# First group's weight preparation reordered: ACT's raising and beginning of a weight put behind the step's activations, DVE's lower part put ahead of the join

## Chip, cores and metric

The kernel runs on one core of one Trainium2 chip. The metric is the time of one execution on the device, in microseconds (us). A program has one instruction queue for each engine: PE (matmuls), ACT, DVE, POOL, and SP, which here issues every DMA. An engine works its queue strictly in order, so an instruction that waits holds up all that stand behind it.

## What is computed

Attention with a window and block summaries, then a feed-forward layer on its result. Cut to what matters:

```python
# q, k, v: (4, 8, 768, 64); w_in: (512, 2048); w_out: (2048, 512); all float32
k_sum = k.reshape(B, H, 24, 32, D).max(axis=3)
v_sum = v.reshape(B, H, 24, 32, D).mean(axis=3)
scores = concat([where(|i - j| < 16, scale * q @ k.T, -1e9),
                 scale * q @ k_sum.T + log(32)], axis=-1)
x = (softmax(scores) @ concat([v, v_sum])).reshape(3072, 512)   # heads side by side
h = x @ w_in
out = (h * tanh(softplus(h))) @ w_out                            # (3072, 512)
```

Each float32 matmul is made of three faster ones, on operands that are split into a rounded high part and a low remainder: high by high, low by high, high by low.

## The kernel before

**Groups and steps.** The 3072 tokens are worked in six groups of 512. A group takes 16 steps, one for each slice of 128 of the 2048 inner columns. Step i, counted over all groups, runs `ff_in` for slice i (12 matmuls into one PSUM tile `ph`, L406), its activation `a` on ACT (`ff_act`, L413), the split of `a` into `ah` (by ACT in the first group, L422) and `al` (by DVE, L424), and `ff_out` for slice i-2 (12 matmuls `po`, L434), which reads `ah` and `al` of two steps before. PE also does the attention of the next group in between: in steps 0, 4, 8 and 12 of the first group the scores (`sc`, L311), in steps 3, 7, 11 and 14 the transposes `pt_ps` (L359), which ACT copies to `pt` (L361), and in steps 4, 8, 12 and 15 the products with the values, `x_ps` (L391), which read `pt`. Of the scores DVE makes `pr` and `nm` (eight instructions, L333), ACT the exponentials (eight, L337); one step later DVE takes the reciprocals `rs` (L347, L348) and POOL multiplies `pr` by them (L351). The exponentials and `a` use different ACT tables, so ACT loads a table on each change.

**Weights.** The weights come from memory as 64-bit floats, in 16 pieces of two slices; their order is w_in 0, 2, w_out 0, w_in 4, w_out 2, w_in 6, w_out 4, and so on, up to w_out 14. Here they are called pieces 0 to 15 (13 is w_in 14, 14 is w_out 12, 15 is w_out 14). Each goes through five small functions, one call of each in a step of the first group:

- `load_weight`: two DMAs of 512 KB into one of two staging tiles `w`; it waits until the piece two before has left that tile.
- `begin_weight`: ACT makes `f` (L136), DVE makes `x` (L138, L140), both from the staging tile.
- `join_weight`: DVE joins `f` and `x` in place (L148, L150).
- `upper_weight`: ACT rounds `f` to `w_hi` (L158).
- `lower_weight`: DVE makes `w_lo` = `f` - `w_hi` (L165).

The order is written by hand: the scheduler keeps the order in which the loop at L514 calls them, on each engine. Step i begins piece i+4, loads piece i+6 and joins piece i+3. Before the change it raises and lowers piece i+2, so that the raise at the head of step i waits for the join of step i-1. The last begin is in step 11, the last join in step 12. What SP issues in a step besides the weight are loads for the attention of later steps: `qk`, `vw` and `vm` in steps 4, 8, 12, and the sources `vsum` and `ks` of the summaries, one after the other through a single buffer (`ks` is read by DVE's `km`, L244, in steps 4, 6, 8, 10; `vsum` by `vq`, L264, in steps 5, 7, 9, 11).

Of the kernel before, what the change touches and what calls it, by code (L numbers as in the profile page):

```python
# [58 lines left out]
def fused_kernel(ctx: ExitStack, tc: tile.TileContext, q0, qk, kt, v0, vw, vs, w_in, w_out, out):  # L59
# [46 lines left out]
    def home(j, part, dtype, name):  # L106

        if j == NW:
            t = stage.tile([P, WB, WP], I64, tag="stage", name=name).bitcast(dtype)
            return t.rearrange("p k f -> p (k f)")[:, :WB * WP]  # L110
        pool = const if j < EARLY else late[0]
        return pool.tile([P, WB * WP], dtype, tag=f"w{part}_{j}", name=name, bufs=1)
# [6 lines left out]
    def load_weight():  # L119
        if weights:  # L120
            w, fc = weights.pop(0)
            t = stage.tile([P, WB, WP], I64, tag="stage", name=f"w{w}_{fc}")
            for k in range(WB):
                nc.sync.dma_start(t[:, k, :], (w_in, w_out)[w][fc + k])
            loaded.append((w, fc, t))

    def begin_weight():
        if loaded:
            w, fc, t = loaded.pop(0)
            j = order[w, fc]  # L130
            flat = t.rearrange("p k f -> p (k f)")
            high = flat.bitcast(U32).rearrange("p (f two) -> p f two", two=2)[:, :, 1]
            quarter = flat.bitcast(U16).rearrange("p (f four) -> p f four", four=4)
            x = home(j, 0, U32, f"x{w}_{fc}")
            f = home(j + 1, 1, F32, f"f{w}_{fc}")
            nc.scalar.activation(f, high.bitcast(F32), AF.Copy, scale=2.0 ** -OFFSET)  # L136
            half = x.bitcast(U16).rearrange("p (f two) -> p f two", two=2)
            nc.vector.tensor_scalar(out=half[:, :, 0], in0=quarter[:, :, 1], scalar1=13, scalar2=None,  # L138
                                    op0=ALU.logical_shift_right)
            nc.vector.tensor_scalar(out=half[:, :, 1], in0=quarter[:, :, 3], scalar1=SIGN, scalar2=None,  # L140
                                    op0=ALU.bitwise_and)
            begun.append((w, fc, f, x))

    def join_weight():
        if begun:
            w, fc, f, x = begun.pop(0)
            u = f.bitcast(U32)
            nc.vector.tensor_scalar(out=f, in0=f, scalar1=-_as_f32(F32_MAX), scalar2=_as_f32(F32_MAX),  # L148
                                    op0=ALU.max, op1=ALU.min)
            nc.vector.scalar_tensor_tensor(out=u, in0=u, scalar=3, in1=x,  # L150
                                           op0=ALU.logical_shift_left, op1=ALU.bitwise_or)
            joined.append((w, fc, f))

    def upper_weight():
        if joined:
            w, fc, f = joined.pop(0)
            split[w, fc, 0] = home(order[w, fc], 0, F32R, f"w{w}_{fc}_hi")
            nc.scalar.copy(split[w, fc, 0], f)  # L158
            raised.append((w, fc, f))

    def lower_weight():
        if raised:
            w, fc, f = raised.pop(0)
            split[w, fc, 1] = home(order[w, fc], 1, F32R, f"w{w}_{fc}_lo")
            nc.vector.tensor_sub(split[w, fc, 1], f, split[w, fc, 0].bitcast(F32))  # L165
# [177 lines left out]
    def att_normalize(group):  # L343
        n = len(group) * NQ
        u = units[group[0]]
        rs = small.tile([P, 2 * NQ], F32, tag="rs", name=f"rs{group[0][0]}_{group[0][1]}")[:, :n]
        nc.vector.tensor_scalar_add(rs, u["sm"][:, :n], 1e-9)  # L347
        nc.vector.reciprocal(rs, rs)  # L348
        if u.get("squares"):
            nc.gpsimd.memset(u["wide"][:, :, KA:], 0.0)  # L350
        nc.gpsimd.tensor_mul(u["pr"], u["pr"], rs.unsqueeze(2).broadcast_to([P, n, KA]))  # L351
# [23 lines left out]
    def att_values(group):  # L375
        c, hp0 = group[0]
        n = len(group)
        g, half = divmod(c, CG)
        if g not in xs:
            xs[g] = (xp.tile([P, HP, TG], F32R, tag="xh", name=f"xh{g}"),  # L380
                     xp.tile([P, HP, TG], F32R, tag="xl", name=f"xl{g}"))
        xh, xl = (x[:, hp0:hp0 + n, half * CH:(half + 1) * CH] for x in xs[g])
        ps = att_psum(c, f"x_ps{c}_{hp0}")
        for k, unit in enumerate(group):
            u = units.pop(unit)
            for s in range(NQ):
                for h in range(2):
                    d = slice(h * D, (h + 1) * D)
                    x = ps[d, k * CH + s * QT:k * CH + (s + 1) * QT]
                    pt = u["pt"][:, h * NQ // 2 + s // 2, s % 2 * QT:(s % 2 + 1) * QT]  # L390
                    nc.tensor.matmul(x, u["v"][:, s, d], pt, start=True, stop=True)  # L391
        x = ps[:, :n * CH].rearrange("p (k t) -> p k t", k=n)
        nc.scalar.copy(xh, x)  # L393
        return lambda: nc.vector.tensor_sub(xl, x, xh.bitcast(F32))  # L394
# [5 lines left out]
    def ff_in(g, fc):  # L400
        xh, xl = xs[g]
        ph = ps_w.tile([P, TG], F32, tag="w", name=f"ph{g}_{fc}")
        wh, wl = (weight(0, part, fc) for part in range(2))
        for cc in range(NCC):
            for n, (w, x) in enumerate(((wh, xh), (wh, xl), (wl, xh))):
                nc.tensor.matmul(ph, w[:, cc * P:(cc + 1) * P], x[:, cc, :],  # L406
                                 start=(cc == 0 and n == 0), stop=(cc == NCC - 1 and n == 2))
        st[g, fc] = ph

    def ff_act(g, fc):  # L410

        a = ff.tile([P, TG], F32, tag="t", name=f"a{g}_{fc}", bufs=2)
        nc.scalar.activation(a, st[g, fc], AF.Mish)  # L413
        st[g, fc] = a

    def ff_split(g, fc):

        a = st[g, fc]
        ah = ff.tile([P, TG], F32R, tag="ah", name=f"ah{g}_{fc}")
        al = ff.tile([P, TG], F32R, tag="al", name=f"al{g}_{fc}")  # L420

        (nc.scalar.copy if g == 0 else nc.vector.tensor_copy)(ah, a)  # L422
        st[g, fc] = ah, al
        return lambda: nc.vector.tensor_sub(al, a, ah.bitcast(F32))  # L424
# [87 lines left out]
    turned = {i + (3 if i < NFC - 4 else 2): group for i, group in at.items() if i < NFC - 1}  # L512
    following = dict(zip(turns, (at[i] for i in turns[1:])))
    for i in range(len(steps) + 2):  # L514
        upper_weight()
        join_weight()
        begin_weight()
        load_weight()
        if i - 1 in at and i < NFC:
            att_normalize(at[i - 1])  # L520
        if i < len(steps):
            ff_in(*steps[i])
            ff_act(*steps[i])
            if i < NFC:
                split_rest = ff_split(*steps[i])
        group = values.get(i)
        lower = att_values(group) if group else None
        if lower and i >= NFC:
            lower()
        if i in at:  # L530
            att_scores(at[i], i >= NFC - 1)
        lower_weight()
        if i < NFC:
            if lower:
                lower()
            split_rest()
        if i - 1 in at and i >= NFC:
            att_normalize(at[i - 1])
        if i - 3 in at and i - 3 >= NFC - 1:
            att_transpose_blocks(at[i - 3], 1)  # L540
        if NFC <= i < len(steps):
            ff_split(*steps[i])()
        if i - 2 in at and i - 2 >= NFC - 1:
            att_transpose_blocks(at[i - 2], 0)
        if i - 3 in following:
            n, m = following[i - 3]
            att_summarize_values(*m)
            after = todo.index(m) + 1
            if after < len(todo) and todo[after][0] % CPB == 0:
                load_key_source(todo[after][0] // CPB, todo[after][1])  # L550
        if i in following:
            n, m = following[i]
            att_summarize_keys(*n)
            for unit in (n, m):
                att_load_keys(*unit)
        if i - 1 in following:
            n, m = following[i - 1]
            att_summarize_values(*n)
            if m[0] % CPB == 0:
                load_key_source(m[0] // CPB, m[1])  # L560
        if i - 2 in following:
            n, m = following[i - 2]
            att_summarize_keys(*m)
            for unit in (n, m):
                att_block_keys(*unit)
        if group:
            for unit in at.get(i, ()):
                att_load_values(*unit)
        if i >= 2:
            ff_out(*steps[i - 2])  # L570
        if i in turned:
            att_transpose(turned[i])
# [44 lines left out]
```

## Time and profile before

| what | before |
|---|---|
| median of 3 runs | 634.47 us (633.5 to 635.5) |
| profiled execution, its own time | 633.05 us |
| its span, first to last instruction | 630.9 us |
| mean granted TensorE clock | 0.99 |
| PE matmul busy | 604.1 us, 96% of the span |
| DVE busy | 385.8 us, 61% |
| ACT busy | 258.8 us, 41% |
| POOL busy | 78.7 us, 12% |
| DMA | 69.26 MB, 110 GB/s over the span |

How to read it: busy shares are means over stages that differ. The span has a lead-in of some 45 us, the first group, which prepares the weights beside its own work, and five more groups in which the weights lie ready. Only the first group's steps are changed.

### The profile page before, as it was taken

To read this page: it belongs to the slowest core of one execution; us is meant where nothing else is said; L and a number is where in the kernel's file an instruction comes from. 1 tells how busy PE (TensorE), PEld (TensorE's weight loads), DVE (VectorE), ACT (ScalarE), POOL (GpSimd) and SP (SyncE) were. 2 spreads that over 40 slices of the span, in tenths; PEclk is the share of its full clock that TensorE was granted. 3 is DMA by queue.
4 is the path that set the end of the run, shared out by engine and by line. 5 is a ranking of instruction groups with operands and counts; after the bars stand their busy time and mean duration, and the time that the engine had idled before them with its cause. 6 is when DMAs were issued, how large, how long until landed. Compare 5 with 4: busy or idle time off the path is not lost.

```text
span 630.9 us, 10795 instructions
## 1 busy us (share of the span) xinstructions
PE 604.1 (96%) x4096; PEld 495.1 (78%) x4096; DVE 385.8 (61%) x1032; ACT 258.8 (41%) x630; POOL 78.7 (12%) x119
## 2 busy tenths in 40 slices
PE   5859999799999999999999999999999999999997
PEld 4747887588888888788888888888888888888886
DVE  4678999982855667855656758756647636222221
ACT  3759867675334244245144244153253251111111
POOL 4441020221011011011011010110110110000000
PEclk9979999999999999999999999999999999999999
DMA  8957587733223043533033241532232010100001
GB/s 273 319 191 249 215 271 238 220 115 97 92 72 122 2 146 122 169 98 97 0 98 96 92 147 55 169 99 88 75 97 82 16 33 0 68 0 1 0 1 66
DMA packets 31779, 69.26 MB, mean 110 GB/s; under 512 B 4720, under 2 KB 11120, under 8 KB 31728
## 3 DMA queue, kind: packets, MB, share of 16 engines
q1 hardware_dynamic: 31728, 68.58, 34.2%
q8 instruction: 32, 0.52, 0.4%
q14 instruction: 19, 0.16, 0.1%
HBM read 60.16 MB, written 6.29 MB: 105 GB/s over the span
## 4 chain that ended last, share of the span: by engine, by line
PE 78%; DMA 7%; DVE 7%; ACT 3%; issue 2%; SPq 1%; POOL 0%; DVEq 0%; ACTq 0%; POOLq 0%
PE po L434 37%; PE ph L406 35%; DMA vw<-vw 3%; PE x_ps L391 3%; PE sc L311 3%; DMA w<-w_out 2%; DMA w<-w_in 1%; DVE w_lo L165 1%; DVE al L424 1%; DVE x L138 1%; ACT f L136 1%; ACT pr L337 1%; DVE x L140 1%; DVE f L148 1%; DMA ks<-kt 1%
## 5 line engine op out<-in xcount | busy, mean ns | idle before, releaser
L413 ACT ACTIVATE a<-ph 128x512 f32<-128x512 f32 x96 | 57.2, 596 | 284.1 <-PE ph L406 230.6
L434 PE MATMUL po<-w_hi,ah 128*128 128x512 f32 x384 | 152.0, 396 | 0.7 <-ACT ah L422 0.5
L434 PE MATMUL po<-w_hi,al 128*128 128x512 f32 x384 | 149.9, 390 | 1.4 <-DVE al L424 1.4
L406 PE MATMUL ph<-xh,w_hi 128*128 128x512 f32 x384 | 150.7, 393 | 0.0
L406 PE MATMUL ph<-xl,w_hi 128*128 128x512 f32 x384 | 150.2, 391 | 0.0
L406 PE MATMUL ph<-xh,w_lo 128*128 128x512 f32 x384 | 150.0, 391 | 0.0
L434 PE MATMUL po<-w_lo,ah 128*128 128x512 f32 x384 | 149.6, 390 | 0.0
L422 DVE CAST ah<-a 128x512 fp32r<-128x512 f32 x80 | 34.6, 433 | 144.1 <-ACT a L413 143.6
L372 DVE STREAM_TRANSPOSE pt<-pr 32x256 f32<-32x256 f32 x256 | 111.5, 436 | 3.6
L434 PEld LDWEIGHTS po<-w_hi,ah 128*128 128x128 f32 x384 | 72.1, 188 | 19.0 <-issue 3.0
L434 PEld LDWEIGHTS po<-w_hi,al 128*128 128x128 f32 x384 | 72.1, 188 | 16.7 <-DVE al L424 2.5
L406 PEld LDWEIGHTS ph<-xh,w_hi 128*128 128x128 f32 x384 | 72.6, 189 | 15.2 <-issue 0.2
L406 PEld LDWEIGHTS ph<-xh,w_lo 128*128 128x128 f32 x384 | 72.5, 189 | 15.2
L406 PEld LDWEIGHTS ph<-xl,w_hi 128*128 128x128 f32 x384 | 72.5, 189 | 14.9
L434 PEld LDWEIGHTS po<-w_lo,ah 128*128 128x128 f32 x384 | 72.1, 188 | 15.2
L337 ACT ACTIVATE pr<-pr,nm 128x120 f32<-128x120 f32 x192 | 73.2, 383 | 14.8 <-DVE nm L333 14.6
L351 POOL TENSOR_TENSOR pr<-pr,rs 128x960 f32<-128x960 f32 (+1 forms) x28 | 47.4, 1692 | 221.8 <-DVE rs L348 131.8
L424 DVE TENSOR_TENSOR al<-a,ah 128x512 fp32r<-128x512 f32 x96 | 69.7, 726 | 5.9 <-ACT ah L422 3.1
L391 PEld LDWEIGHTS x_ps<-pt,vw 120*64 120x64 f32 x768 | 25.7, 141 | 21.3 <-issue 8.6
L391 PE MATMUL x_ps<-pt,vw 120*64 120x64 f32 x768 | 29.4, 229 | 12.7 <-ACT pt L361 5.4
L394 DVE TENSOR_TENSOR xl<-x_ps,xh 128x512 fp32r<-128x512 f32 (+1 forms) x28 | 17.2, 614 | 34.9 <-ACT xh L393 34.5
L337 ACT ACTIVATION_READ_ACCUMULATOR pr<-pr,nm 128x1 f32 x192 | 35.9, 187 | 0.0
(59 smaller groups left out, 451.4 us busy)
## 6 DMA issues: line engine op xcount, KB each, us to landing
qk<-qk SPq DMA_DIRECT2D x40, 496.0 KB, 4.1
vw<-vw SPq DMA_DIRECT2D x48, 192.0 KB, 5.1
w<-w_in SPq DMA_DIRECT2D x16, 512.0 KB, 5.2
w<-w_out SPq DMA_DIRECT2D x16, 512.0 KB, 5.2
ks<-kt SPq DMA_DIRECT2D x16, 384.0 KB, 4.4
out<-o SPq DMA_DIRECT2D x24, 256.0 KB, 2.3
vsum<-vs SPq DMA_DIRECT2D x12, 384.0 KB, 3.4
vw<-vm SPq DMA_DIRECT2D x40, 48.0 KB
```

Of the source, the lines that this page charges most:

```text
L136: nc.scalar.activation(f, high.bitcast(F32), AF.Copy, scale=2.0 ** -OFFSET)
L311: nc.tensor.matmul(ps[h][row, at0:at0 + KA], u["qk"][r, s, h * QT:(h + 1) * QT], u["qk"][r, s, P:], start=True, stop=True)
L337: nc.scalar.activation(pr[:, j, :], pr[:, j, :], AF.Exp, scale=-1.0, bias=nm[:, j:j + 1], accum_out=sm[:, j:j + 1])
L351: nc.gpsimd.tensor_mul(u["pr"], u["pr"], rs.unsqueeze(2).broadcast_to([P, n, KA]))
L372: nc.vector.transpose(u["tr"][b * SQ:(b + 1) * SQ, :, a * SQ:(a + 1) * SQ], u["wide"][a * SQ:(a + 1) * SQ, :, b * SQ:(b + 1) * SQ])
L391: nc.tensor.matmul(x, u["v"][:, s, d], pt, start=True, stop=True)
L394: return lambda: nc.vector.tensor_sub(xl, x, xh.bitcast(F32))
L406: nc.tensor.matmul(ph, w[:, cc * P:(cc + 1) * P], x[:, cc, :], start=(cc == 0 and n == 0), stop=(cc == NCC - 1 and n == 2))
L413: nc.scalar.activation(a, st[g, fc], AF.Mish)
L422: (nc.scalar.copy if g == 0 else nc.vector.tensor_copy)(ah, a)
L424: return lambda: nc.vector.tensor_sub(al, a, ah.bitcast(F32))
L434: nc.tensor.matmul(po[g][t], a[:, tok], w, start=(fc == 0 and n == 0), stop=(fc == NFC - 1 and n == 2))
```

## The change

Three calls move within the body of the step loop; the functions themselves stay as they are.

```diff
     for i in range(len(steps) + 2):
-        upper_weight()
+        lower_weight()
         join_weight()
-        begin_weight()
-        load_weight()
         if i - 1 in at and i < NFC:
             att_normalize(at[i - 1])
         if i < len(steps):
...
         if i in at:
             att_scores(at[i], i >= NFC - 1)
-        lower_weight()
+        begin_weight()
+        load_weight()
+        upper_weight()
         if i < NFC:
             if lower:
                 lower()
```

After it, a step's ACT work is: activation, `ah`, the copy of `x_ps`, the exponentials, then `f` of piece i+4 and the raise of piece i+3, which waits for the join of the same step. DVE starts a step with the lower part of piece i+2, then joins piece i+3, takes the reciprocals and the scores, and only then makes `x` of piece i+4. The load of piece i+6 stands at the same place in SP's queue as before.

The first place is on ACT, around the end of step 11 (`a_11`; numbers of heads and of w_in or w_out are left out of the names: the first `w_14_hi` is piece 13, `w_12_hi` piece 14, `f_14_1443` piece 15). Before:

```order
L158 CAST w_14_hi<-f_14_1339 128x1024
L136 ACTIVATE f_14_1443<-w_14_1343 128x1024
L413 ACTIVATE a_11_1460<-ph_11_1447 128x512
L422 CAST ah_11_1462<-a_11_1460 128x512
L361 COPY pt_0_1485<-pt_ps_0_1486 120x512
L361 COPY pt_0_1485<-pt_ps_1_1492 120x512
L158 CAST w_12_hi<-f_12_1395 128x1024
L413 ACTIVATE a_12_1515<-ph_12_1502 128x512
L422 CAST ah_12_1517<-a_12_1515 128x512
```

And the same stretch of ACT's queue with the change:

```order
L158 CAST w_14_hi<-f_14_1363 128x1024
L413 ACTIVATE a_11_1457<-ph_11_1444 128x512
L422 CAST ah_11_1459<-a_11_1457 128x512
L136 ACTIVATE f_14_1463<-w_14_1367 128x1024
L158 CAST w_12_hi<-f_12_1415 128x1024
L361 COPY pt_0_1487<-pt_ps_0_1488 120x512
L361 COPY pt_0_1487<-pt_ps_1_1494 120x512
L413 ACTIVATE a_12_1517<-ph_12_1504 128x512
L422 CAST ah_12_1519<-a_12_1517 128x512
```

The activation of step 11 has moved ahead of one `f`; the two copies of the transposes have moved behind that `f` and behind the raise of piece 14. Steps 3 and 7 read the same.

The second place is on DVE, from the end of step 0's scores into step 1 (`w_0_lo` is piece 2, `w_4_lo` piece 3, `f_2` and `x_2` piece 4, `x_6` piece 5). Before:

```order
L165 TENSOR_TENSOR w_0_lo<-f_0_651,w_0_hi 128x1024
L424 TENSOR_TENSOR al_0_736<-a_0_733,ah_0_735 128x512
L148 TENSOR_SCALAR f_2_713<-f_2_713 128x1024
L150 SCALAR_TENSOR_TENSOR f_2_713<-f_2_713,x_2_712 128x1024
L138 TENSOR_SCALAR x_6_786<-w_6_701 128x1024
L140 TENSOR_SCALAR x_6_786<-w_6_701 128x1024
L347 TENSOR_SCALAR rs_0_794<-sm_0_758 128x8
L348 RECIPROCAL rs_0_794<-rs_0_794 128x8
L165 TENSOR_TENSOR w_4_lo<-f_4_697,w_4_hi 128x1024
L424 TENSOR_TENSOR al_1_814<-a_1_811,ah_1_813 128x512
```

And with the change:

```order
L138 TENSOR_SCALAR x_2_769<-w_2_655 128x1024
L140 TENSOR_SCALAR x_2_769<-w_2_655 128x1024
L424 TENSOR_TENSOR al_0_730<-a_0_727,ah_0_729 128x512
L165 TENSOR_TENSOR w_4_lo<-f_4_697,w_4_hi 128x1024
L148 TENSOR_SCALAR f_2_770<-f_2_770 128x1024
L150 SCALAR_TENSOR_TENSOR f_2_770<-f_2_770,x_2_769 128x1024
L347 TENSOR_SCALAR rs_0_788<-sm_0_752 128x8
L348 RECIPROCAL rs_0_788<-rs_0_788 128x8
L138 TENSOR_SCALAR x_6_810<-w_6_701 128x1024
L140 TENSOR_SCALAR x_6_810<-w_6_701 128x1024
L424 TENSOR_TENSOR al_1_808<-a_1_805,ah_1_807 128x512
```

The lower part of piece 3 (`w_4_lo`), which stood at the end of step 1, now stands at its head, ahead of the join, the reciprocals and the begin; and behind the reciprocals stands a begin where a lower part stood.

## The prediction

> **What bounds the kernel now.** First the busy time by stage (columns: from:to, length, then busy time and instructions of PE, PE's weight loads, DVE, ACT, POOL; granted clock, DMA share, GB/s), for the first group and the stretch behind it:
>
> ```profile
> 39.00:128.00 89.00, 79.95 (x562) 64.38 (x563) 82.97 (x148) 66.72 (x120) 14.22 (x12) 0.94 0.69 229
> 128.00:255.00 127.00, 127.00 (x835) 104.54 (x834) 80.09 (x235) 55.53 (x145) 17.22 (x22) 1.00 0.31 99
> ```
>
> From 128 us on PE has no gap: the time is when PE comes through its last wait of the first group, plus a fixed amount of matmuls. In the group DVE is the fullest, 83 of 89 us. Then what PE waits for there (waits, 39 to 130 us: total, times, longest), and the rows of the two `x_ps` in PE's timeline (start, length):
>
> ```profile
> PE x_ps L391 <- ACT pt L361: 4.3, 2, 2.8
> PE po L434 <- DVE al L424: 1.4, 2, 1.2
> ...
> 96.27 1.18 PE L391 MATMUL x_ps<-pt,vw 120*64 120x64 f32 x32 [1.54 <-ACT pt L361]
> 125.57 1.17 PE L391 MATMUL x_ps<-pt,vw 120*64 120x64 f32 x32 [2.77 <-ACT pt L361]
> ```
>
> The last wait is that of step 12's `x_ps`, which starts at 125.57. It sets the end; waits before it count only as far as they reach it. ACT's timeline shows what was ahead of it:
>
> ```profile
> 119.56 1.06 ACT L158 CAST w_hi<-f 128x1024 fp32r<-128x1024 f32 x1 [3.74 <-DVE f L150]
> 122.78 1.12 ACT L136 ACTIVATE f<-w 128x1024 f32<-128x1024 f32 x1 [2.16 <-DMA w<-w_out]
> ...
> 124.94 1.06 ACT L361 COPY pt<-pt_ps 120x512 f32<-120x512 f32 x2
> 126.54 1.05 ACT L158 CAST w_hi<-f 128x1024 fp32r<-128x1024 f32 x1 [0.54 <-DVE f L150]
> ```
>
> ACT is not short of time: it waits for DVE's join of step 10, then for piece 15's DMA, and the copies `pt` come behind both. The raise at 126.54 waits for step 11's join and stands behind the copies.
>
> **The change, part by part.** The sum follows when the copies of step 11 can run.
>
> *Step 0 to 1.* DVE before, and ACT before:
>
> ```profile
> 49.96 0.69 DVE L148 TENSOR_SCALAR f<-f 128x1024 f32<-128x1024 f32 x1 [0.85 <-ACT f L136]
> ...
> 53.12 0.26 DVE L333 CUSTOM_DVE_ANT_0 pr<-sc,base 128x120 f32<-128x120 f32 x1
> ...
> 54.73 1.22 DVE L165 TENSOR_TENSOR w_lo<-f,w_hi 128x1024 fp32r<-128x1024 f32 x1
> 55.86 0.68 DVE L424 TENSOR_TENSOR al<-a,ah 128x512 fp32r<-128x512 f32 x1
> 56.47 0.68 DVE L148 TENSOR_SCALAR f<-f 128x1024 f32<-128x1024 f32 x1
> ...
> 58.33 0.78 DVE L138 TENSOR_SCALAR x<-w 128x1024 uint16<-128x1024 uint16 x1
> ...
> 59.65 0.15 DVE L347 TENSOR_SCALAR rs<-sm 128x8 f32<-128x8 f32 x1
> ...
> 62.61 0.70 DVE L424 TENSOR_TENSOR al<-a,ah 128x512 fp32r<-128x512 f32 x1 [1.50 <-ACT ah L422]
> 63.24 0.75 DVE L148 TENSOR_SCALAR f<-f 128x1024 f32<-128x1024 f32 x1
> ```
> ```profile
> 48.79 2.23 ACT L136 ACTIVATE f<-w 128x1024 f32<-128x1024 f32 x2
> 51.03 1.28 ACT L413 ACT_TABLE_LOAD   x1
> ...
> 53.60 1.28 ACT L337 ACT_TABLE_LOAD   x1
> 54.89 0.40 ACT L337 ACTIVATE pr<-pr,nm 128x120 f32<-128x120 f32 x1
> ...
> 57.94 1.04 ACT L158 CAST w_hi<-f 128x1024 fp32r<-128x1024 f32 x1
> 58.88 1.14 ACT L136 ACTIVATE f<-w 128x1024 f32<-128x1024 f32 x1
> 60.04 1.28 ACT L413 ACT_TABLE_LOAD   x1
> ```
>
> Start to start on DVE: scores 1.61 (53.12 to 54.73), lower 1.13, `al` 0.61, join 1.86, begin 1.32, reciprocals some 0.3. DVE is free at 49.11 (49.96 less its wait). With the change it fills that wait with piece 2's lower part and comes to the end of step 0 at 49.11 + 1.13 + 1.86 + 1.61 + 1.32 + 0.61 = 55.64. Next in its queue is piece 3's lower part, which needs piece 3 raised; and on ACT the raise now stands behind everything of step 0. ACT: `f` of piece 3 ends at 49.9 (half of the 2.23); table, `a`, `ah` 2.57 (51.03 to 53.60); table 1.29; eight exponentials 3.05 (54.89 to 57.94); `f` of piece 4 1.16; the raise 0.94: done at 58.9. **DVE stands idle for 3.2 us**, with the join, the reciprocals and everything behind them. Step 1 then takes 1.13 + 1.86 + 0.3 + 1.32 + 0.61 = 5.2, and the multiplication on POOL, below, adds 1.6: it ends at 65.7. Before, it ended at 63.24, with a wait of 1.50 for `ah` that now goes. **DVE is 2.4 us later.**
>
> *POOL beside the begin.* What follows the reciprocals on DVE runs beside POOL's L351:
>
> ```profile
> 84.77 2.57 POOL L351 TENSOR_TENSOR pr<-pr,rs 128x960 f32<-128x960 f32 x1 [20.66 <-DVE rs L348]
> 85.61 2.28 DVE L424 TENSOR_TENSOR al<-a,ah 128x512 fp32r<-128x512 f32 x1
> ...
> 32.74 0.61 POOL L227 COPY vw<-vm 24x512 f32<-24x512 f32 x1
> 32.90 1.07 DVE L138 TENSOR_SCALAR x<-w 128x1024 uint16<-128x1024 uint16 x1
> ```
>
> At 85.61 `al` took 2.28 instead of 0.68: it was held until POOL ended, 1.6 us lost. With the change the begin's two instructions stand there. Are they held too? The one at 32.90, issued while POOL copied, took 1.07 instead of 0.78, as if held until the copy ended. So I charge 1.6, as before; in steps 5 and 9 that changes nothing. Were they free to run, POOL would be nearly through before `al`, and each of steps 1, 5 and 9 would cost about 1.2 us less. The Trainium skill speaks to this (SBUF — State Buffer, Who interferes with whom): a `tensor_scalar` in a mode that uses two ports, or an instruction with two inputs in SBUF, blocks against GpSimd for the whole instruction, and whoever issues first goes first. By that rule the 1.6 stays if the begin's 16-bit strided operands reach such a mode, and else falls by 1.2 three times; the row at 32.90 sides with the first.
>
> *Steps 4 to 5 and 8 to 9.* Again the lower part waits for a raise behind exponentials. From the first score: some 0.3 until the first exponential (estimate), 3.05, `f` 1.16, raise 0.94: 5.4. DVE has 1.61 + 1.32, `xl` and `al` at 0.61 each, and `km` at 0.9: 5.0. **0.4 us each**; together 0.8. In step 12 the wait falls behind the point that decides.
>
> *The load behind the exponentials.* `f` now frees the staging tile late. In steps 4 and 8 the next load of 1 MB is issued 0.5 us ahead of `km`'s end, at whose end SP issues `vsum`, `qk`, `vw`, `vm`, and, after them and one more weight, the `ks` that `km` reads two steps on. Before, it came at the step's head and was out of the way. SP and DVE:
>
> ```profile
> 81.15 0.34 SPq L205 DMA_DIRECT2D vsum<-vs  x1
> ...
> 94.44 0.95 DVE L244 TENSOR_REDUCE km<-ks 128x24 f32<-128x768 f32 x1 [0.33 <-DMA ks<-kt]
> ...
> 109.61 0.33 SPq L205 DMA_DIRECT2D vsum<-vs  x1
> ...
> 123.69 0.95 DVE L244 TENSOR_REDUCE km<-ks 128x24 f32<-128x768 f32 x1 [1.16 <-DMA ks<-kt]
> ...
> 44.00:48.00 4.00, 4.00 (x23) 3.31 (x24) 3.40 (x5) 0.53 (x2) 0.00 (x0) 0.50 0.91 313
> ```
>
> Both `km` wait for that burst already, by 0.33 and 1.16. At 313 GB/s for a share of 0.91, 1.05 MB more takes 3.0 us; less the 0.5 of earlier issue and DVE's own 0.4, each wait grows by 2.1 at most, and by nothing if the weight fits gaps. I take **1.5 each, 3.0 together**, nearer the upper end, since both already wait. Behind `km` on DVE stands the next join.
>
> *The copies of step 11.* They now stand behind the raise of piece 14, which waits for step 11's own join:
>
> ```profile
> 124.56 0.68 DVE L148 TENSOR_SCALAR f<-f 128x1024 f32<-128x1024 f32 x1
> ...
> 126.42 0.76 DVE L138 TENSOR_SCALAR x<-w 128x1024 uint16<-128x1024 uint16 x1
> ```
>
> Before, the join ended at 126.42, with `pt` long copied. Now DVE's step 11 starts 2.4 + 0.8 + 3.0 = 6.2 later, its lower part of 1.13 comes first: the join ends at 133.75. Raise 0.94, first copy 0.6, hand-overs 0.1: **`x_ps` starts at 135.4 instead of 125.57, 9.8 later.** PE gets no cover: step 8's `x_ps`, by the same steps, comes near 104 (96.27 before), and the work between the two takes 25 us, so PE is there by 130 and idles 5 to 6 us.
>
> *The clock.* So long a gap may cool PE:
>
> ```profile
> 40.00:44.00 4.00, 1.51 (x15) 1.01 (x12) 3.05 (x5) 2.83 (x4) 1.85 (x2) 0.50 0.02 4
> ...
> 48.00:52.00 4.00, 4.00 (x44) 2.99 (x44) 3.12 (x5) 3.98 (x4) 0.00 (x0) 0.90 0.23 45
> ...
> 122.00:126.00 4.00, 1.23 (x18) 0.77 (x18) 2.81 (x4) 3.19 (x5) 0.51 (x1) 1.00 0.13 30
> ```
>
> After the thin stretch before 44 the clock was 0.50, through the row of 44 to 48 above and to about 48.8 (0.90 means 0.8 us more): 3.8 us of work at half speed, 1.9 lost. The gap of 2.77 left it at 1.00. For 5 to 6 us I take 0.8, between nothing and 1.9, as the 2 us of small matmuls that come first gain little from the clock. The Trainium skill (TensorE: Matmul & The Clock Gate, What's actually happening) has the clock halve after an idle window of about 3.4 us; by that the 0.8 holds, by the row of 2.77 alone it would go.
>
> Sum: 2.4 + 0.8 + 3.0 + 3.6 (9.8 less 6.2) + 0.8 = 10.6. The profiled execution's own 633.05 (span 630.9 and 2.15 around it) becomes 643.7; the median is 1.4 above it, so **645**. The rest costs nothing: weights are raised earlier than before and lowered a step or more ahead of their use.
>
> **Rivals.** *Smaller loss.* The begin is not held by POOL (-3.6) and the DMA does not matter (-3.0, and no cold clock, -0.8): +3.2, 637.7; with the DMA alone gone, 642. For it: the waits were short; against: the rows at 32.90, 94.44 and 123.69. *Larger loss.* Both `km` waits at 2.1 or a little above, the full 1.9 of clock, and a further wait of a similar size: about 649. *Faster.* ACT's activations come one `f` earlier and no longer behind a weight's DMA (2.16 at 122.78); were the join done when ACT reaches the raise, PE's waits of 4.3 and 1.4 would go: 628.8. It decides on whether DVE runs ahead of ACT, and the 3.74 at 119.56 says that it doesn't. *No difference.* DVE wins back what it loses, by its waits of 0.85 and 1.50, and the copies fall into PE's slack: it would need PE two steps behind DVE.
>
> **How the numbers follow.** Forecast (641.5 to 648, say) 0.60; smaller loss 0.22; larger 0.09; faster 0.05; no difference 0.04. Range 639 to 649: it leaves out the faster and equal cases and the ends of the others. A measurement of this kernel can tell about 0.3%, 1.9 us, from no change: slower 0.91, same 0.04, faster 0.05.
>
> **What would show it.** Right: DVE's `w_lo` waits for ACT's `w_hi` by about 3 us near 56; ACT's `w_hi` waits for DVE's `f` by some 3 to 5 us in most steps; PE waits for `pt` three times, 3 to 6 us each, the last ending near 135; `km` waits for `ks` by 2 us or so near 99 and 130; clock below 1.00 behind 135. Wrong: `pt` copied in steps 7 and 11 ahead of the raise's wait, or DVE at step 11's join no later than 126.

## The result and the profile after

The changed kernel is slower: 642.27 us (641.97 to 645.94, 4 runs) against 634.61 (633.5 to 635.5, 4 runs), a ratio of 1.0135 [1.0095, 1.0175]. Run again beside the later experiments it took 643.91 (642.94 to 644.71, 4 runs) against 633.72 (25 runs), 1.0166 [1.0127, 1.0205]. The forecast was 645, range 639 to 649.

The first profiled execution is the slowest of its four (645.94, span 644.2). Its busy time by stage (columns as in the prediction):

```profile
39.00:128.00 89.00, 75.00 (x473) 60.52 (x474) 77.97 (x141) 62.86 (x116) 15.52 (x14) 0.85 0.65 219
128.00:255.00 127.00, 125.51 (x852) 103.14 (x852) 81.28 (x219) 53.97 (x131) 15.23 (x21) 1.00 0.30 96
```

Up to 128 us PE was busy 5 us less than before (79.95) and DVE 5 us less (82.97), and the granted clock was 0.85, not 0.94. What they waited for between 39 and 140 us (total, times, longest):

```profile
ACT w_hi L158 <- DVE f L150: 23.4, 8, 5.3
...
PE x_ps L391 <- ACT pt L361: 7.8, 3, 6.0
...
DVE w_lo L165 <- ACT w_hi L158: 4.2, 3, 3.4
...
PE po L434 <- DVE al L424: 3.9, 1, 3.9
...
DVE km L244 <- DMA ks<-kt: 3.3, 2, 2.6
```

ACT's raise waits for DVE's join, DVE's lower part waits for ACT's raise, and PE waits for both. DVE's timeline shows where it lost time (with it the POOL multiplication of step 1):

```profile
61.69 1.23 DVE L165 TENSOR_TENSOR w_lo<-f,w_hi 128x1024 fp32r<-128x1024 f32 x1 [3.37 <-ACT w_hi L158]
...
65.25 2.10 POOL L351 TENSOR_TENSOR pr<-pr,rs 128x960 f32<-128x960 f32 x1 [20.66 <-DVE rs L348]
65.62 2.33 DVE L140 TENSOR_SCALAR x<-w 128x1024 uint16<-128x1024 uint16 x1
...
68.51 1.28 DVE L165 TENSOR_TENSOR w_lo<-f,w_hi 128x1024 fp32r<-128x1024 f32 x1
...
86.80 1.23 DVE L165 TENSOR_TENSOR w_lo<-f,w_hi 128x1024 fp32r<-128x1024 f32 x1 [0.42 <-ACT w_hi L158]
...
94.56 1.22 DVE L264 TENSOR_REDUCE vq<-vsum 96x32 f32<-96x1024 f32 x1 [0.89 <-DMA vsum<-vs]
...
103.51 0.95 DVE L244 TENSOR_REDUCE km<-ks 128x24 f32<-128x768 f32 x1 [2.64 <-DMA ks<-kt]
...
119.09 1.23 DVE L165 TENSOR_TENSOR w_lo<-f,w_hi 128x1024 fp32r<-128x1024 f32 x1 [0.42 <-ACT w_hi L158]
...
132.87 0.95 DVE L244 TENSOR_REDUCE km<-ks 128x24 f32<-128x768 f32 x1 [0.68 <-DMA ks<-kt]
133.74 1.21 DVE L165 TENSOR_TENSOR w_lo<-f,w_hi 128x1024 fp32r<-128x1024 f32 x1
```

Each wait of the prediction's sum is there: 3.37 in step 1, then 0.42 in steps 5 and 9, `km` on `ks` twice, and the begin's second instruction held to 2.33 beside POOL's multiplication. The `vq` wait of 0.89 was not in the sum. ACT at the two places that PE waits for last, and PE's `x_ps` and its one long wait for `al`:

```profile
107.56 1.05 ACT L158 CAST w_hi<-f 128x1024 fp32r<-128x1024 f32 x1 [3.85 <-DVE f L150]
108.51 1.06 ACT L361 COPY pt<-pt_ps 120x512 f32<-120x512 f32 x2
...
136.92 1.05 ACT L158 CAST w_hi<-f 128x1024 fp32r<-128x1024 f32 x1 [3.35 <-DVE f L150]
137.87 1.07 ACT L361 COPY pt<-pt_ps 120x512 f32<-120x512 f32 x2
```
```profile
46.69 1.12 PE L391 MATMUL x_ps<-pt,vw 120*64 120x64 f32 x16 [1.99 <-issue]
...
68.64 0.79 PE L434 MATMUL po<-w_hi,al 128*128 128x512 f32 x1 [3.86 <-DVE al L424]
...
109.14 1.98 PE L391 MATMUL x_ps<-pt,vw 120*64 120x64 f32 x32 [5.95 <-ACT pt L361]
...
138.50 1.17 PE L391 MATMUL x_ps<-pt,vw 120*64 120x64 f32 x32 [1.49 <-ACT pt L361]
```

In steps 7 and 11 the copies `pt` start as soon as the raise ahead of them ends, and the raise waited 3.85 and 3.35 for the join of its own step. The row at 46.69 is the last `x_ps` of the lead-in, before at 43.96: the lead-in, whose code is the same, was 2.73 us later in this execution. So I measure a **stage** from that `x_ps` to the one of step 12: 81.61 us before (43.96 to 125.57), 91.81 after. The rest is nearly the same: `x_ps` of step 15 comes 19.58 behind that of step 12, 19.53 before. From that `x_ps` of step 15 to the end of the execution's time each of the fourteen profiles here takes 487.7 to 488.0 us, so lead-in, stage and the stretch from step 12 to 15 hold all that differs.

### The profile page after: what moved, and what is told of

It is laid out like the page before. It is cut to its first block, busy times and chain, and to the rows that moved or that the text cites. A ratio compares the mean times of both kernels' runs of the same rounds, so it can differ in the third digit from the quotient of the medians.

```text
span 644.2 us, 10799 instructions
## 1 busy us (share of the span) xinstructions
PE 610.1 (95%) x4096; PEld 500.4 (78%) x4096; DVE 388.2 (60%) x1032; ACT 259.3 (40%) x630; POOL 77.3 (12%) x119
## 4 chain that ended last, share of the span: by engine, by line
PE 78%; DVE 9%; ACT 5%; DMA 4%; issue 3%; SPq 1%; POOL 0%; DVEq 0%; POOLq 0%; ACTq 0%
PE po L434 36%; PE ph L406 34%; PE x_ps L391 4%; PE sc L311 3%; ACT pr L337 2%; DVE w_lo L165 2%; DMA ks<-kt 2%; DMA vw<-vw 1%; DMA qk<-qk 1%; DVE f L150 1%; DVE f L148 1%; DVE x L140 1%; ACT w_hi L158 1%; ACT f L136 1%; DVE x L138 1%
## 5 line engine op out<-in xcount | busy, mean ns | idle before, releaser
L351 POOL TENSOR_TENSOR pr<-pr,rs 128x960 f32<-128x960 f32 (+1 forms) x28 | 44.6, 1594 | 228.5 <-DVE rs L348 111.6
L424 DVE TENSOR_TENSOR al<-a,ah 128x512 fp32r<-128x512 f32 x96 | 67.1, 699 | 5.4 <-ACT ah L422 2.7
L391 PE MATMUL x_ps<-pt,vw 120*64 120x64 f32 x768 | 30.9, 236 | 16.0 <-ACT pt L361 9.6
L333 DVE CUSTOM_DVE_ANT_0 pr<-sc,base 128x120 f32<-128x120 f32 x128 | 31.5, 276 | 7.5 <-PE sc L311 6.6
```

Of the source, the lines that this page charges most:

```text
L333: nc.vector.tensor_tensor_reduce(out=pr[:, j, :], in0=ps[h][:, at0:at0 + KA], in1=m, scale=-SCALE, scalar=-NEG, op0=ALU.add, op1=ALU.min, ...
```

## Experiments

Each ratio is to the kernel before on the same chip; its median was 634.61 for the first row of the table, 633.63 for the second to fifth, 633.17 for the sixth to ninth, 633.72 for the last four. The expectations of the four runs that undo one part count the stage from the first `ph`, 1.05 us later than I do here.

| run | median us | ratio to before | stage | step 12 to 15 | wait ahead of step 12's `x_ps` |
|---|---|---|---|---|---|
| changed, first profile | 642.27 | 1.0135 [1.0095, 1.0175] | 91.81 | 19.58 | 1.49 |
| lower part back | 640.45 | 1.0101 [1.0066, 1.0135] | 87.74 | 21.09 | 3.66 |
| begin and load back | 642.04 | 1.0126 [1.0093, 1.0159] | 87.68 | 21.89 | 3.52 |
| raise back | 639.34 | 1.0075 [1.0048, 1.0102] | 85.59 | 20.78 | 1.65 |
| load at the step's end | 643.18 | 1.0145 [1.0114, 1.0177] | 88.60 | 21.12 | 2.86 |
| raise alone | 637.07 | 1.0050 [1.0028, 1.0073] | 83.10 | 21.11 | 3.59 |
| begin and load alone | 636.52 | 1.0040 [1.0013, 1.0066] | 81.84 | 19.58 | 0.85 |
| lower part alone | 637.75 | 1.0069 [1.0045, 1.0092] | 83.42 | 21.03 | 2.92 |
| lower a step later, begin early | 631.22 | 0.9965 [0.9944, 0.9985] | 79.34 | 19.55 | 1.66 |
| changed, again | 643.91 | 1.0166 [1.0127, 1.0205] | 90.43 | 21.07 | 3.09 |
| the same, and `vq` early | 631.35 | 0.9962 [0.9939, 0.9985] | 79.83 | 21.07 | 2.27 |
| raise alone, wait filled | 635.89 | 1.0037 [1.0015, 1.0058] | 83.49 | 19.55 | 0.43 |
| lower a step later, alone | 634.20 | 1.0001 [0.9977, 1.0025] | 80.53 | 19.54 | 1.59 |

"The same, and `vq` early" goes with "lower a step later, begin early". The theory: DVE and ACT work for each other within one step (join, raise, then both the copies and the lower part), so each is held by the other's other work. The rivals: the loads that come late, and the begin beside POOL.

**The changed kernel again.** No edit.

> The changed kernel once more, for a second profile of it and a time beside those of the other runs. Its first profile had its lead-in, which the change does not touch, 2.7 us later than that of before, and its stage 10.2 us longer. If the stage's 10.2 belongs to the change, a profile with an ordinary lead-in (last x_ps of it near 44 to 45) shows step 12's x_ps near 54 + 82 = 134.5 to 136, and the median is 641 to 643. If a part of the 10.2 came from that one execution's lateness, x_ps stands below 134.5. Waits as before: DVE w_lo on w_hi about 3.4 once, ACT w_hi on f 3 to 5 us, POOL-held begins of 2.3.

("54 + 82" is a slip of the pen: 44 to 45 and the stage's 91 are meant.) Its profiled execution took 644.71 (span 643.0). First PE, then DVE:

```profile
45.34 1.12 PE L391 MATMUL x_ps<-pt,vw 120*64 120x64 f32 x16 [1.97 <-issue]
...
67.30 0.50 PE L434 MATMUL po<-w_hi,al 128*128 128x512 f32 x1 [3.26 <-DVE al L424]
...
106.21 1.98 PE L391 MATMUL x_ps<-pt,vw 120*64 120x64 f32 x32 [4.35 <-ACT pt L361]
...
135.77 1.22 PE L391 MATMUL x_ps<-pt,vw 120*64 120x64 f32 x32 [3.09 <-ACT pt L361]
```
```profile
67.17 1.28 DVE L165 TENSOR_TENSOR w_lo<-f,w_hi 128x1024 fp32r<-128x1024 f32 x1
...
92.20 1.21 DVE L264 TENSOR_REDUCE vq<-vsum 96x32 f32<-96x1024 f32 x1
...
100.57 0.95 DVE L244 TENSOR_REDUCE km<-ks 128x24 f32<-128x768 f32 x1 [2.07 <-DMA ks<-kt]
...
130.13 0.95 DVE L244 TENSOR_REDUCE km<-ks 128x24 f32<-128x768 f32 x1 [0.89 <-DMA ks<-kt]
131.00 1.21 DVE L165 TENSOR_TENSOR w_lo<-f,w_hi 128x1024 fp32r<-128x1024 f32 x1
```

The lead-in was 1.38 later than before and the stage took 90.43, so the stage's loss, 8.8 and 10.2 us in the two profiles, is the change's own and not the lateness of one lead-in; the median, 643.91, came out somewhat above the 641 to 643 that I expected. The waits on DMAs differ between the two executions (`vq` none here, `km` 2.07 instead of 2.64), and here the last wait of PE was 3.09 and the clock fell behind it.

**One part undone.** Lower part back behind the scores:

```diff
-        lower_weight()
         join_weight()
...
+        lower_weight()
         begin_weight()
         load_weight()
         upper_weight()
```

> The changed kernel with DVE's lower part put back behind the scores (the begin and the raise stay late). Theory: three separate terms add up, and the lower part ahead of the join is one of them: DVE's wait for the raise at the head of steps 1, 5 and 9 (3.37, 0.42, 0.42 us in the changed kernel's trace) shrinks to under 2 us in all, and the join of step 11 no longer has 1.13 us ahead of it. From the first ph to step 12's x_ps 90.8 us in the changed kernel, 80.6 before: here 86 to 87. Time 637 to 639 us against 642.3. Rival (only the copies behind the raise matter): 641 or more, since that order stays. Rival (only the loads behind the exponentials matter): 641 or more.

Begin and load back behind the join:

```diff
         join_weight()
+        begin_weight()
+        load_weight()
...
-        begin_weight()
-        load_weight()
         upper_weight()
```

> The changed kernel with begin and load put back to the head of the step. Theory: f no longer stands between the exponentials and the raise, so DVE's wait at the head of step 1 falls from 3.37 to about 2.2 us, and the weight's load is out of the attention loads' way: km's waits for ks fall from 2.64 and 0.68 to under 1 each, vq's 0.89 goes. First ph to step 12's x_ps 85.5 to 87; time 637 to 639. Rival (the lower part alone): DVE's wait stays above 3 us, time 641. Rival (copies alone): 641 or more.

Raise behind the transposes and their copies, at the end of the step, which is the place it had before:

```diff
-        upper_weight()
...
             att_transpose(turned[i])
+        upper_weight()
```

> The changed kernel with the raise put behind the copies of the transposes, at the end of the step. Theory: the copies of steps 3, 7 and 11 no longer wait for their own step's join; step 12's x_ps then follows the activation of step 11, some 3 to 4 us earlier, while DVE's wait of some 3.4 us at step 1 and the waits for ks stay as they are. First ph to step 12's x_ps 86.5 to 88; time 638 to 640. Rival (the loads or the lower part carry all): no gain, 642.

Load alone to the end of the step:

```diff
-        load_weight()
...
             att_transpose(turned[i])
+        load_weight()
```

> The changed kernel with the weight's load issued at the end of the step, behind the attention loads of SP, nothing else moved. Theory: km's waits for ks (2.64 and 0.68) and vq's for vsum (0.89) shrink to under 1.5 us in all, as the 1 MB no longer stands ahead of them; DVE comes 2 to 3 us earlier to step 11; first ph to step 12's x_ps 88 to 89, time 639.5 to 641. Rival (DMA sharing is even, so order on SP's queue does not matter): waits as in the changed kernel, time 642.

With the lower part or the begin back the stage shortened as expected, by about 4 us against the first profile and 2.7 against the second. The time shortened less: 640.45 and 642.04, where 637 to 639 was expected; 642.04 is where the rivals of that run put it (641 or more), and DVE's wait in step 1 stayed at 3.40 in it, as one of them had it, where 2.2 was expected. PE then waited 3.66 and 3.52 ahead of step 12's `x_ps`, and step 15's came 21.1 and 21.9 behind it instead of 19.5. The raise gave the most: its time was as expected, its stage shorter than expected (its 20.78 holds a wait of 0.86 of PE for POOL). Only its ratio lies clear of the changed kernel's second one; for the other two the times alone do not tell a gain from noise. The load at the end took the waits of `km` and `vq` away and shortened the stage of its profile by 1.8 to 3.2, but the median, 643.18, did not improve (639.5 to 641 was expected). The weights now came late themselves; ACT in that run:

```profile
125.97 1.17 ACT L136 ACTIVATE f<-w 128x1024 f32<-128x1024 f32 x1 [5.82 <-DMA w<-w_out]
```

A row like it, also with 5.82, stands at 96.76. So the first rival's waits are real, but a later place for the load alone does not mend them: they move to the weights.

**One part alone**, each against the kernel before. Raise:

```diff
-        upper_weight()
         join_weight()
...
         lower_weight()
+        upper_weight()
```

> One of the three moves alone: only the raise goes behind the scores (and so behind the exponentials); begin and load stay at the step's head, the lower part behind the scores. The pairs so far lost, between the last x_ps of the lead-in and that of step 12, 6.1 us (raise and begin), 6.1 (raise and lower part) and 4.0 (lower part and begin), all three together 10.2. If the moves simply add up, the pairs give 4.0 us for the raise and 2.0 for each of the others: the stage takes 85.6 and the time is about 637.5. Rival: each move alone falls into slack and only two of them together lose: stage within 1 us of 81.6, time 633 to 635. In both, DVE's lower part waits for ACT's w_hi some 1 to 3 us in a few steps, and the copies pt stand behind the raise as in the changed kernel.

Begin and load:

```diff
         join_weight()
-        begin_weight()
-        load_weight()
...
         lower_weight()
+        begin_weight()
+        load_weight()
```

> One move alone: only begin and load go behind the scores; raise and join stay at the head, the lower part behind the scores. If the moves add up: 2.0 us, stage 83.6, time about 635.5. If the charge of POOL holding the begin (2.3 instead of 0.8 us) and the late load are each worth what I charged and reach the end, 3 to 4 us: stage 85 to 86, time 637 to 638. Rival: it falls into slack, 633 to 635. In all cases the begin's second instruction takes 2.3 us beside POOL's multiplication, and no lower part waits for w_hi.

Lower part:

```diff
         upper_weight()
+        lower_weight()
         join_weight()
...
-        lower_weight()
```

> One move alone: only the lower part goes to the head of the step, right behind the raise's issue and ahead of the join; nothing else moves. If the moves add up: 2.0 us, stage 83.6, time about 635.5. If DVE, with the lower part ahead of the join, waits for the raise in every step (1.0 us of ACT each), and the raise of the next step waits for the later join in turn, 3 us and more: time 636.5 to 638. Rival: within 0.3% of before, 633 to 635, since DVE is not held by exponentials here.

None falls into slack: by the ratios, whose intervals all lie above 1, they cost 0.5, 0.4 and 0.7%, together 1.6%, where all three at once cost 1.35 and 1.66%. So by the medians they roughly add up, though not in the 4, 2 and 2 us that I had worked out from the stages of the runs above: the time was as expected only for the raise. The waits were not all as expected either: with the raise alone no lower part waited for a raise, and the lower part alone waited for one in three steps, not in every step. For the raise alone and the lower part alone the profiles show most of it: stages 1.5 and 1.8 longer, and 1.6 and 1.5 more behind step 12. For begin and load the profile does not show it: that execution was the shortest of its ten (633.35 of 633.35 to 637.84), its stage only 0.2 longer. Where its other executions lose 3 us stays open. The begins beside POOL were held there too, at their first instruction and not at their second as expected (2.34, 2.37, 2.34). In the kernel before, `al` is held in the same place in steps 5 and 9 (2.28 at 85.61 and again at 114.04), and in step 1 it waited 1.50 for `ah`; so holding the begin instead need not make the stage longer, and in that execution it hardly did.

**The clock.** The raise alone, and twelve more matmuls ahead of step 12's `ff_in`, which fill most of PE's last wait:

```diff
+        for _ in range(12 if (g, fc) == (0, 12) else 0):
+            nc.tensor.matmul(ph, wh[:, :P], xh[:, 0, :], start=True, stop=True)
         for cc in range(NCC):
```

> The order with the raise alone moved back, and ahead of step 12's first matmul the same matmul 12 times more, into a tile that the real ones then overwrite: 2.7 us of PE work in place of most of the 3.6 us wait. If the 1.6 us that this order loses behind step 12's x_ps come from the clock that fell in that wait (0.79 in 128 to 136 us), the granted clock stays at 1.00, x_ps of step 15 comes 19.5 behind that of step 12 instead of 21.1, and the time falls by 1 to 1.6 us to about 635.5 to 636 in spite of the added work. If the loss has another cause, or the wait is not what lowers the clock: 637 or more, 21 us as before.

The window from 128 to 136 us of the raise alone, then of the run with the wait filled:

```profile
128.00:136.00 8.00, 8.00 (x76) 6.53 (x72) 7.93 (x26) 6.52 (x21) 0.00 (x0) 0.79 0.47 160
```
```profile
128.00:136.00 8.00, 8.00 (x88) 6.67 (x83) 7.93 (x25) 6.50 (x22) 0.00 (x0) 1.00 0.45 151
```

With more work on PE the kernel was no slower, 635.89 against 637.07 (the intervals of the ratios overlap, so the times alone would not settle it); the clock stayed at 1.00, and step 15's `x_ps` came 19.55 behind step 12's, not 21.11. A wait that lets the clock fall costs some 1.5 us on top of itself.

**Lower part a step later.** At the head of the step, but ahead of the raise, so that it takes the weight raised one step earlier:

```diff
+        lower_weight()
         upper_weight()
         join_weight()
...
-        lower_weight()
```

> The lower part at the head of the step, ahead of the raise instead of behind it; begin and load stay where they were before. It differs from the run with the lower part alone moved in one place only: each lower part takes the weight raised one step earlier, and so waits for nothing. If that wait within one step is what cost 4 us there, this one is back at 632 to 634, the stage at 80.5 to 82, with no w_lo behind w_hi. If the place ahead of the join costs, whatever the lower part waits for: 636 or more, stage 83 and above.

It differs from "lower part alone" in the order of two neighbouring lines. There DVE had waits like the first row, of 3.42 and twice 0.66, and raises waited behind the join; here, in the second row, DVE is early enough to wait for `ah`:

```profile
59.65 1.23 DVE L165 TENSOR_TENSOR w_lo<-f,w_hi 128x1024 fp32r<-128x1024 f32 x1 [3.42 <-ACT w_hi L158]
```
```profile
62.03 0.69 DVE L424 TENSOR_TENSOR al<-a,ah 128x512 fp32r<-128x512 f32 x1 [3.52 <-ACT ah L422]
```

The ratio goes from 1.0069 [1.0045, 1.0092] to 1.0001 [0.9977, 1.0025]. The stage, 80.53, is as expected, the time, 634.20, 0.2 above. So it is not the place ahead of the join that costs, but the wait for a raise of the same step, with what follows from it. One such consequence is in the first of the two profiles: late as DVE was, the lower part of step 2 there ran into POOL's multiplication and took 2.82,

```profile
64.79 2.82 DVE L165 TENSOR_TENSOR w_lo<-f,w_hi 128x1024 fp32r<-128x1024 f32 x1
```

while in the second one it came behind that multiplication and took 1.22.

**A version that beats both.** Begin and load, besides, behind the activation:

```diff
+        lower_weight()
         upper_weight()
         join_weight()
-        begin_weight()
-        load_weight()
...
                 split_rest = ff_split(*steps[i])
+        begin_weight()
+        load_weight()
...
-        lower_weight()
```

> A try to beat both: the lower part at the head of the step ahead of the raise, so that it takes the weight raised a whole step earlier and waits for nothing; then raise and join; begin and load behind the activations and the first half of the split, ahead of the scores. If the loss comes from DVE and ACT waiting for each other within one step, this order has no such wait (no w_lo behind w_hi, ACT w_hi behind f under 3 us): stage 79.5 to 81, time 631.5 to 633. Rival: the last wait of PE, for the copies of step 11 behind the raise, remains as it was: stage 81.6, time 633 to 635. Second rival: begin and load ahead of the scores delay the exponentials by the 1.3 us of begin in every step: stage 83 and more, time over 635.

```profile
120.74 0.60 ACT L413 ACTIVATE a<-ph 128x512 f32<-128x512 f32 x1
121.37 0.62 ACT L422 CAST ah<-a 128x512 fp32r<-128x512 f32 x1
121.89 1.12 ACT L136 ACTIVATE f<-w 128x1024 f32<-128x1024 f32 x1
122.92 1.05 ACT L361 COPY pt<-pt_ps 120x512 f32<-120x512 f32 x2
```

631.22 us, all ten runs between 630.49 and 632.34. In the kernel before, `f` of piece 15 stood ahead of `a` and waited 2.16 for its DMA, and the copies came at 124.94; here `a` and `ah` fill that time, `f` has no wait, and the copies come at 122.92, 2.0 earlier. The stage is 2.3 shorter, so stage and time came out slightly below what I expected (79.5 and 631.5). No lower part waits for a raise; ACT's raise still waits for the join, by up to 3.8 where under 3 was expected.

The begins beside POOL are still held there (2.36, 2.35, 2.37). The last run puts the summary `vq` of steps 5 and 9, with the load behind it, right after the reciprocals, ahead of those begins, so that `vq` runs beside POOL's multiplication in their stead:

```diff
             att_normalize(at[i - 1])
+        if i - 1 in following and i < NFC:
+            n, m = following[i - 1]
+            att_summarize_values(*n)
+            if m[0] % CPB == 0:
+                load_key_source(m[0] // CPB, m[1])
...
-        if i - 1 in following:
+        if i - 1 in following and i >= NFC:
```

> The faster order (lower part ahead of the raise, a step later; begin and load behind the activations), and in it the summary vq, 1.2 us of DVE, moved from the end of steps 5 and 9 to their start, right behind the reciprocals, where POOL multiplies. If vq, a reduction, is not held by POOL, it covers the 1.6 us that the begin's second instruction now stands held (2.36, 2.35, 2.37), in steps 5 and 9: 1.2 to 1.6 us less on DVE each, of which 1 to 2 reach step 12: stage 77.5 to 78.5, time 629.5 to 630.5. If vq is held as well, or waits for its DMA vsum, nothing is won: stage 79.3 or more, time 631 to 632.

```profile
83.00 1.79 POOL L351 TENSOR_TENSOR pr<-pr,rs 128x960 f32<-128x960 f32 x1 [21.81 <-DVE rs L348]
83.99 1.22 DVE L264 TENSOR_REDUCE vq<-vsum 96x32 f32<-96x1024 f32 x1 [1.16 <-DMA vsum<-vs]
85.24 0.18 DVE L265 TENSOR_SCALAR vq<-vq 96x32 f32<-96x32 f32 x1
85.33 0.77 DVE L138 TENSOR_SCALAR x<-w 128x1024 uint16<-128x1024 uint16 x1
85.98 0.76 DVE L140 TENSOR_SCALAR x<-w 128x1024 uint16<-128x1024 uint16 x1
```

`vq` is not held (1.22), and the begin behind it is free (0.76), but `vq` waits for its own DMA, by 1.16 here and 0.30 in step 9. The time, 631.35, is that of the second case: no gain on the version above. In this profile the clock also fell in the wait of 2.27 ahead of step 12's `x_ps`, and step 15's came 21.07 behind it instead of 19.55; how much of the missing gain is the DMA and how much the clock stays open.

## Why the prediction was right, step by step

The prediction's sum, and the same terms in the two profiles of the changed kernel, in us, each less the lateness of that execution's lead-in (2.73 and 1.38). "DVE late" is taken at the first DVE instruction of step 2, before at 63.24, and of step 11, before at 124.56; the rows between make 6.10 and 4.84 of the latter, and some 0.2 to 0.4 is spread over other rows.

| term | predicted | first profile | second |
|---|---|---|---|
| DVE late at the end of step 1 | 2.4 | 68.51 - 63.24 - 2.73 = 2.54 | 67.17 - 63.24 - 1.38 = 2.55 |
| lower part in steps 5 and 9 | 0.8 | 0.84 | 0.82 |
| waits for late loads | 3.0 | 2.31 - 0.48 + 0.89 = 2.72 | 1.74 - 0.27 = 1.47 |
| DVE late at the start of step 11 | 6.2 | 6.45 | 5.06 |
| lower part, then copies behind their own step's raise | 3.6 | 10.20 - 6.45 = 3.75 | 8.82 - 5.06 = 3.76 |
| clock behind step 12's `x_ps` | 0.8 | 19.58 - 19.53 = 0.05 | 21.07 - 19.53 = 1.54 |
| sum | 10.6 | 10.25 | 10.36 |

- *Step 0 to 1.* Right: an idle of 3.2 us of DVE forecast, 3.37 and 3.39 measured.
- *POOL beside the begin.* Right: 2.33, 2.36 and 2.35 us instead of 0.76. The Trainium skill (SBUF — State Buffer, Who interferes with whom) lets a `tensor_scalar` in a two-port mode block against GpSimd for the whole instruction, and a `tensor_reduce` never on this chip. The traces agree, by the 2.33 here and the 1.22 of the early `vq`; that the begin's instructions run in such a mode no run shows directly.
- *The loads.* The sum was nearly right, its parts were not: not 1.5 on each `km`, but most of it in step 6, a shorter wait than before in step 10 (0.68 for 1.16), and in one of two executions a wait of `vq`. This term changes much from one execution to the next, and in the second it was half of what was charged.
- *The copies of step 11.* Right, to 0.2.
- *The waits of PE.* This sign was wrong. PE was to wait three times for `pt`, by 3 to 6 us each. It waited 0.40, 5.95 and 1.49, and 1.45, 4.35 and 3.09 in the second profile. I had left out that PE meets DVE's lateness first in step 2, at `al` (3.86 and 3.26), and that this takes most of the wait of step 4.
- *The clock.* Right in kind, wrong in place. Behind the last wait it stayed up in the first profile and fell in the second:

```profile
136.00:144.00 8.00, 6.51 (x84) 5.17 (x83) 7.93 (x20) 5.60 (x11) 0.00 (x0) 1.00 0.27 81
```
```profile
136.00:144.00 8.00, 8.00 (x84) 6.63 (x81) 7.09 (x24) 6.52 (x22) 0.00 (x0) 0.79 0.58 182
```

The clock also fell in the earlier waits, as these windows of the first profile show (granted clock third from the end):

```profile
68.00:72.00 4.00, 3.36 (x8) 2.68 (x9) 3.97 (x5) 0.70 (x2) 0.56 (x2) 0.50 0.62 242
...
108.00:112.00 4.00, 2.86 (x52) 2.74 (x56) 3.96 (x7) 3.51 (x7) 0.00 (x0) 0.50 0.47 152
```

From step 8's `x_ps` to the wait ahead of step 12's, PE took 27.87 us (109.14 to 137.01) there and 26.47 in the second profile (106.21 to 132.68); before, by the two `x_ps` rows of the prediction, 26.53, and not the 25 that it used. So in the first profile PE came 1.4 us later to the last wait. That wait ended with the copies, which stood behind DVE's join, so the delay cost nothing; and the wait shrank to 1.49, behind which the clock stayed up. In the second profile the wait was 3.09 and the loss 1.54 us. The 0.8 lies between two cases, neither of which has that value, and the reason given for it does not hold: the 32 small matmuls of one `x_ps` took 1.98 in the row at 109.14, at a clock of 0.50, and 1.17 at 138.50, at 1.00, so they lose much by a low clock.
- *From span to median.* Here lies the error of the 645. Less the lateness of their lead-ins the two executions took 643.2 and 643.3, and 643.7 was forecast; the step of 1.4 to the median of before was added to it. But the medians of the changed kernel were 642.27 and 643.91, not above its profiled executions. A forecast against one execution carries that execution's lead-in with it, and here the lead-in's last `x_ps` was found between 43.41 and 46.69 in fourteen profiles, all with the same code up to there.

That the sums, 10.25 and 10.36, come so close to 10.6 is in part luck: in the first profile the clock gave 0.75 less than charged and the loads 0.3 less, against small excesses elsewhere; in the second the loads gave 1.5 less and the clock 0.7 more.

The rivals fell where the text said they would: the smaller loss needed begins that are not held, the faster case a DVE that runs ahead of ACT, and ACT's raise waited for DVE eight times. One variant of the smaller loss, with the loads alone costing nothing, was put at 642, beside the 642.27 measured. The profiles speak against it, with 2.72 and 1.47 us of such waits; what the loads cost in the executions without a profile is not known.

That begin with load, lower part and raise each cost by themselves, and that for the lower part the cause is that it takes a weight raised in the same step, is shown by runs. That the held begins and the late loads cost what the sum gives them is read from the profiles; no run took away one of them alone without moving another wait.

## What to carry to other kernels

When two engines prepare something in turns, let each take what the other finished a step earlier: the same instruction at the same place cost 0.7% when it took the product of its own step and nothing when it took the one before. What is moved behind a long block of other work on its engine (here eight exponentials and two table loads) is late by the whole block, and so is everything that the other engine has queued behind its wait. Follow the lateness to the last wait of the bound engine; waits ahead of that one may be long and cost nothing.

## What the hardware showed beside that

Ahead of step 12's `x_ps` eight of the fourteen profiles have a wait of 2.27 us or more, and in seven of them step 15's came 21.0 to 21.9 us later instead of 19.5; the eighth is the kernel before, whose 2.77 left the clock at 1.00, while 2.27 in the last version let it fall. So the length of the wait alone does not decide. The Trainium skill (TensorE: Matmul & The Clock Gate, What's actually happening) has the clock set by free-running windows of about 3.4 us; an effect of where a wait falls agrees with these rows, though waits below 3.4 were enough in several.
